# A recurrent state attention with two networks behind it on one core: transforms folded once more, the recurrence's heads laid out anew by partition halves

## The chip, the cores and the metric

One core of a Trainium2 chip runs the whole program. The metric is device time in microseconds (us). The engines are named as the profile names them: PE is TensorE's matmuls, PEld its weight loads, DVE is VectorE, ACT is ScalarE, POOL is GpSimd, SP is SyncE, whose queue issues most of the DMAs here.

## What is computed

```python
# 4 batches x 8 heads, 768 tokens, head dimension 40: 32 independent recurrences
for t in range(768):
    y[:, :, t] = einsum('bhd,bhde->bhe', r_t, state)
    Sa = einsum('bhde,bhe->bhd', state, a_t)
    state = state * w_t[:, :, None, :] - einsum('bhd,bhe->bhde', Sa, b_t) + einsum('bhd,bhe->bhde', v_t, k_t)
x = y, as [4, 768, 320]
# first network
u  = x + Re(FFT over tokens and features of x)
un = (u - mean(u)) / sqrt(var(u) + 1e-6)
x  = u + relu(un @ w_ch1) @ w_ch2                      # 320 -> 1280 -> 320
# second network
u  = x + transpose(relu(transpose(x) @ w_tok1) @ w_tok2)  # tokens 768 -> 256 -> 768
out = u + relu(u @ w_ch1) @ w_ch2                      # 320 -> 1536 -> 320
```

Precision is float32. Many products are made of high and low parts of the operands (names that end in `h` and `l`), as several matmuls that add up in one PSUM tile.

## The kernel before

**The recurrence.** The 768 tokens are cut into 12 superchunks of 64. Within a superchunk the recurrence becomes a triangular system for each of the 32 heads: `load`, `decay` (two scans on VectorE) and `kg` (score products, masked, written to `RT` and `LT`) prepare it. For each pair of superchunks, called a round here (6 in all), `inv` inverts the 32x32 triangular diagonal blocks of both superchunks at once on VectorE, with one block on each of 128 partitions: products (line 349) and reductions (line 350) over blocks of 8, 16 and 32. The blocks come from `RT` by way of DRAM: `RT` to `Gd`, `Gd` to the tile `N`. The result `Mt` goes to DRAM as `Md`, and its transposed form `MT`, which ScalarE makes, as `Ad`; they come back as `Mst` (four pieces a superchunk) and `AT`. `merge` joins the two 32-blocks of each head with 32x32 matmuls (`mg`, line 391, and `mc`, line 401) and ScalarE copies.

The serial part is `chain`, once a superchunk. 64 matmuls give `x` from `LT` and `RT` (line 450). Copies by VectorE and ScalarE put it into the block-diagonal tile `bdX`, two heads side by side, in four half-width pieces. 32 matmuls with all 128 rows (as the trace counts them, two for each call of the code) give the solve `z` from `Mst` and `bdX` (line 462). From it follow the new state, which is added to `LT`, and the next superchunk. `outp` makes the outputs of the superchunk and stores them. `wdec` decodes weights beside all this, and small matmuls called `warm` (line 55), whose result nobody reads, are put into TensorE's idle time.

**The Fourier layer.** For each batch, `fft` adds and subtracts mirrored tokens on VectorE (`F`, one folding) and transforms 3 token tiles with `psA` (line 868). `fft2` makes the transform over features, added up as `mix`: 6 tiles of 128 tokens, each 8 matmuls of 320 columns (line 895). Statistics, normalisation and transpositions follow.

**The networks.** They run in groups of 3 token tiles (384 tokens), 8 groups a network. For each of 10 (12) pieces `m` of the hidden width, `hps` is the first product (line 961, 8 matmuls of 384 columns), ScalarE and VectorE turn it into `hh` and `hl`, and `acc` is the second product (line 951, 9 matmuls of 320 columns). The token mixing of the second network is `tok` and `tok2`. Weights arrive packed; DVE, ACT and POOL decode them, the pieces are stored to DRAM (`dr_...`) and loaded again as `k` (first network) and `v` (second) from GpSimd's queue.

**The order.** The program is one list of operations with their dependences, and `Plan.emit` writes out the order on every engine before anything runs. Each operation has an estimated cost and a key, `lst`: the least, over its successors, of their key less (latency + cost) times `SLACK`; some operations have a due time as well, and `OFF` adds an offset for each stage (`inv`, `chain`, `decode` and so on) and for each of its instances. Smaller keys go first. At each step the engine whose next operation can start earliest takes, among those that could start within 0.25 us of that, the one with the least key. PSUM banks are dealt out by the same list: in the networks 2 banks `mm`, 3 `acc` and 3 `ps`.

## Time and profile before

| what | value |
|---|---|
| median of 3 runs | 994.69 us (993.87 to 1008.61) |
| profiled execution | 995.55 us |
| its span | 993.9 us, 24531 instructions |
| PE busy | 961.6 us (97%) |
| PEld busy | 924.0 us (93%) |
| DVE busy | 608.8 us (61%) |
| ACT busy | 420.5 us (42%) |
| POOL busy | 312.3 us (31%) |

The span is the time from the first to the last instruction of the profiled execution; its own time also holds what lies around that. A busy share is an average over stages that are limited by different things, so the rows below are taken by stage. `warm` counts as busy time of PE.

### The profile page before, as it was taken

The page shows a single profiled execution, that of the slowest core. Times are in us where ns is not written, and L with a number is a line of the kernel's source. Part 1 is how long each engine was busy: PE and PEld are TensorE (multiplying, and loading weights), DVE is VectorE, ACT ScalarE, POOL GpSimd, SP SyncE. Part 2 cuts the span into 40 slices and gives each one's busy share as a digit, 9 for nine tenths or more (in the row PEclk, how much of TensorE's full clock was granted, in tenths as well). Part 3 has the DMA queues.
Part 4 walks back from the last instruction along what each step waited for, and adds up shares of the span by engine and source line. Part 5 has one row for each costly group of instructions (what it writes and reads, how often), then busy time and mean ns, then how long its engine had stood idle before and what let it go on. Part 6 is the DMA issues. An engine that isn't in the chain of part 4 may idle for free. (4 is left out here: it accounts for less than half of the span.)

```text
span 993.9 us, 24531 instructions
## 1 busy us (share of the span) xinstructions
PE 961.6 (97%) x10119; PEld 924.0 (93%) x10119; DVE 608.8 (61%) x1364; ACT 420.5 (42%) x870; POOL 312.3 (31%) x427
## 2 busy tenths in 40 slices
PE   9998999999999899999999999999999999999998
PEld 8897788888888799899999999999999999999998
DVE  5699669888786159997798677626252522332322
ACT  4357787775857465423433333214131211221221
POOL 6754567663733255321215244420000000000000
PEclk9999999998999799999999999999999999999999
DMA  9996887889696777631325345491000000000000
GB/s 205 198 224 122 199 213 184 194 222 196 166 211 149 206 189 250 228 116 51 101 87 164 121 132 175 124 403 57 1 20 1 20 1 20 22 20 1 21 21 20
DMA packets 128722, 125.61 MB, mean 126 GB/s; under 512 B 85059, under 2 KB 105987, under 8 KB 128483
## 3 DMA queue, kind: packets, MB, share of 16 engines
q1 hardware_dynamic: 123715, 100.38, 40.0%
q0 software_dynamic: 4896, 23.67, 6.9%
q8 instruction: 79, 1.29, 0.6%
q14 instruction: 32, 0.26, 0.1%
HBM read 85.40 MB, written 33.84 MB: 120 GB/s over the span
## 5 line engine op out<-in xcount | busy, mean ns | idle before, releaser
L964 DVE SCALAR_TENSOR_TENSOR hl<-hps,hh 128x384 fp32r<-128x384 f32 x176 | 98.0, 557 | 234.1 <-ACT hh L963 233.1
L963 ACT ACTIVATE hh<-hps 128x384 fp32r<-128x384 f32 x176 | 86.5, 491 | 320.1 <-PE hps L961 320.0
L961 PE MATMUL hps<-th,v 128*128 128x384 f32 x576 | 142.5, 338 | 0.0
L951 PE MATMUL acc<-v,hh 128*128 128x320 f32 x576 | 128.8, 310 | 0.0
L961 PE MATMUL hps<-th,W 128*128 128x384 f32 x480 | 119.4, 339 | 0.1
L951 PE MATMUL acc<-W,hh 128*128 128x320 f32 x480 | 107.4, 310 | 0.6 <-DMA W<-m11l 0.6
L961 PEld LDWEIGHTS hps<-th,v 128*128 128x128 f32 x576 | 103.8, 188 | 0.2
L951 PEld LDWEIGHTS acc<-v,hh 128*128 128x128 f32 x576 | 97.9, 188 | 0.0
L829 POOL TENSOR_TENSOR mda<-mda,mdh 128x320 f32<-128x320 f32 (+2 forms) x44 | 45.4, 1037 | 149.2 <-DVE mdt L827 84.4
L951 PE MATMUL acc<-v,hl 128*128 128x320 f32 x288 | 89.0, 309 | 0.0
L961 PEld LDWEIGHTS hps<-th,W 128*128 128x128 f32 x480 | 86.8, 188 | 1.3 <-DVE hl L964 0.6
L951 PEld LDWEIGHTS acc<-W,hh 128*128 128x128 f32 x480 | 81.2, 188 | 0.8 <-DMA W<-m11l 0.8
L55 PE MATMUL warm<-ident 128*128 128x128 f32 x590 | 74.4, 282 | 3.0 <-POOL Q L237 2.0
L55 PEld LDWEIGHTS warm<-ident 128*128 128x128 f32 x590 | 70.3, 196 | 4.3 <-POOL Q L237 2.0
L951 PE MATMUL acc<-W,hl 128*128 128x320 f32 x240 | 73.9, 308 | 0.0
L961 PE MATMUL hps<-tl,v 128*128 128x384 f32 x192 | 64.6, 337 | 0.0
L521 PE MATMUL sc<-rm,VZd 120*128 120x192 f32 x264 | 54.2, 345 | 2.7 <-DVE sc L526 1.7
L951 PEld LDWEIGHTS acc<-v,hl 128*128 128x128 f32 x288 | 54.1, 188 | 0.0
L961 PE MATMUL hps<-tl,W 128*128 128x384 f32 x160 | 53.9, 337 | 0.0
L531 POOL TENSOR_SCALAR_AFFINE_SELECT sc<-sc 64x384 f32<-64x384 f32 (+1 forms) x72 | 38.6, 540 | 47.8 <-ACT sc L233 45.5
L311 PE MATMUL kg<-am,bt 120*128 120x192 f32 x242 | 50.2, 346 | 3.5 <-issue 1.8
L521 PEld LDWEIGHTS sc<-rm,VZd 120*128 120x128 f32 x264 | 43.0, 194 | 6.8 <-DVE sc L526 3.0
(176 smaller groups left out, 2025.0 us busy)
## 6 DMA issues: line engine op xcount, KB each, us to landing
bt<-in_bkR_dram SPq DMA_DIRECT2D x12, 660.0 KB
mdraw<-in_moe_w_ch_dram SPq DMA_DIRECT2D x22, 320.0 KB
wS<-in_wR_dram SPq DMA_DIRECT2D x12, 335.2 KB
a<-in_aR_dram SPq DMA_DIRECT2D x12, 335.2 KB
RT<-a SPq DMA_DIRECT2D x36, 111.7 KB
...
```

The costliest lines, as they stand in the source:

```text
L55: for x in range(m): nc.tensor.matmul(t[:,128*(x%4):128*(x%4)+128],lhsT=ident,rhs=ident,start=True,stop=True)
L311: nc.tensor.matmul(ps[:,192*x:192*x+192],lhsT=bt[:,g+x].rearrange("p v t -> p (v t)"),rhs=am[:,:,g+x],start=True,stop=True)
L521: for x,g in enumerate(gs): nc.tensor.matmul(ps[:,192*x:192*x+192],lhsT=VZd[:,g].rearrange("p v t -> p (v t)"),rhs=s.rm[:,:,g],start=True, ...
L531: nc.gpsimd.affine_select(out=o,in_=o,pattern=[[0,3*m],[1,L]],compare_op=ALU.is_gt,fill=0.0,base=0,channel_multiplier=-1)
L829: P.op('POOL',.06+d*.0025,lambda: nc.gpsimd.tensor_tensor(out=g("da").bitcast(F32),in0=g("da").bitcast(F32),in1=g("dh").bitcast(F32),op=AL ...
L951: nc.tensor.matmul(s.pst(acc[x]),lhsT=a[:,sl],rhs=t[w2][w][:,m],start=(m==0 and n==0),stop=(m==MT-1 and n==2))
L961: for n,(l,r) in enumerate(ops): nc.tensor.matmul(ps,lhsT=l,rhs=r,start=n==0,stop=n==7)
L963: s.act(384,lambda: nc.scalar.activation(out=t["hh"][z],in_=s.pst(h),func=AF.Relu),[kp],[('hh',z)],free=[h[0]])
L964: s.dve(.47,lambda: nc.vector.scalar_tensor_tensor(out=t["hl"][z],in0=s.pst(h),scalar=0.0,in1=t["hh"][z].bitcast(F32),op0=ALU.max,op1=ALU. ...
```

## The change

**The Fourier layer.** The token transform is folded twice: the tokens are kept in an order (`TOK`) in which the second mirror also falls on whole tiles, so that 2 token tiles go in and not 3. The feature transform is made for 161 frequencies only, cosine and sine sums side by side: 4 blocks a batch, each 2 matmuls of 384 columns and 6 of 192. The sums and differences that give both mirrored halves are made on VectorE (`DE`). The rows of `w_tok1` and `w_tok2` and the output are permuted on the host to fit.

**The networks.** They run in 6 chunks of 4 tiles (512 tokens), which may hold tiles of two batches (`TILES4`). `acc` has 4 PSUM banks and `ps` 2, `hh` and `hl` have two buffers, `hps` has 512 columns. The transform, mixing and transposition of the following chunk are put in at the middle of a chunk (`mid`). The `k` weights are loaded before the `v` weights.

**The recurrence.** `Gd`, `Md`, `Ad`, `AT` and their DMAs go. Four DMAs a superchunk bring the blocks from `RT` straight into an on-chip tile `Gs`, and three 32x32 block transpositions a round on VectorE give `N` and both forms of the result. `merge` of both superchunks stands right behind `inv`. Each half of the partitions holds 16 heads of both superchunks. `X1` takes the place of `bdX`: two full-width copies in place of four half-width ones, and the solve `z` is 64 matmuls (counted the same way) of 64 rows and 40 columns, which alternate between the upper and the lower 64 rows. Superchunks 0, 1, 6 and 7 are stored in reversed order of time, tables are smaller, and one buffer of `sc` goes.

**The order.** `SLACK` goes from 34.66 to 8 and every offset in `OFF` to 0; the planner's costs get an estimate of instruction fetch and of the hand-over of PSUM tiles, and new DMA constants.

```diff
-SLACK=34.6615
+SLACK=8.0000
+ROW={0:65,1:1,6:449,7:385}
...
+        s.X1,=mk(c2,1,[128,32,D],"X1"); s.Mst=mk(c2,2,[128,32,L],"Mst")
+        s.B,=mk(c2,1,[128,32,32],"B")
...
+        s.N,=mk(e,1,[128,32,32],"N"); s.Mt,=mk(e,1,[128,32,32],"Mt"); s.Gs,=mk(e,1,[128,32,32],"Gs")
...
-        s.Gd=mk(dr,2,[2,2,32,32,32],"Gd"); s.Md=mk(dr,2,[2,2,32,32,32],"Md"); s.Ad=mk(dr,2,[2,32,32,32],"Ad")
...
-        R=i//2
+        R=i//2; x=i%2
         for b in range(2):
-            s.dma(s.Gd[R%2][i%2,b].rearrange("n j t -> j n t"),RT[32*b:32*b+32,0:32,32*b:32*b+32],k6,[('Gd',R%2,i%2,b),('RTg',i%NRT,b)],.9)
-        q=32*(i%4)
-        s.act(.97,s.B[q:q+32],RT[0:32,0:32,32:64],k6,[('B',i%4),('RTg',i%NRT,2)],q=(0,q) if q else 0)
-        x=i%2
-        s.dma(s.N[64*x:64*x+64],s.Gd[R%2][x].rearrange("b n j t -> (b n) j t"),[('Gd',R%2,x,b) for b in range(2)],[('N',x)],.85)
+            for v in range(2):
+                q=64*v+32*b
+                s.dma(s.Gs[q:q+32,16*x:16*x+16],RT[32*b:32*b+32,16*v:16*v+16,32*b:32*b+32],k6,[('Gs',x,b,v),('RTg',i%NRT,b)],.5,ext=-.2)
+        for v in range(2):
+            s.act(.5,s.B[64*v:64*v+32,16*x:16*x+16],RT[0:32,16*v:16*v+16,32:64],k6,[('B',i%2,v),('RTg',i%NRT,2)],q=(0,64*v) if v else 0)
 
...
+        P.op('DVE',1.1,lambda: V.transpose(out=n(0,[1,32],[32,32]),in_=view(s.Gs,0,[1,32],[32,32])),[('Gs',x,b,v) for x in range(2) for b in range(2) for v in range(2)],NK+['S3'],lk=1)
...
-        s.act(.9,s.MT,s.Mt.rearrange("p i j -> p j i"),mk,['MT'])
-        for x in range(2):
-            s.dma(s.Ad[R%2][x],s.MT[64*x:64*x+32],['MT'],[('Ad',R%2,x)],.42)
-        s.dma(s.Md[R%2].rearrange("s b n i t -> (s b n) i t"),s.Mt,mk,[('Md',R%2)],1.69)
+        P.op('DVE',1.1,lambda: V.transpose(out=n(0,[1,32],[32,32]),in_=mm(0,[32,32],[1,32])),mk,NK+['S3'],lk=1)
+        P.op('DVE',1.1,lambda: V.transpose(out=view(s.Mst[R%2],32,[1,32],[L,32]),in_=mm(0,[1,32],[32,32])),mk,[('M',2*(R%2)),('M',2*(R%2)+1)],lk=1)
...
+        nc=s.nc; P=s.P; R=i//2; x0=16*(i%2); Mst=s.Mst[R%2]; B=s.B; km=('M',i%4); kt=('Tm',i%2)
+        for v in range(2): q=64*v; s.act(.48,Mst[q:q+32,x0:x0+16,0:32],Mst[q:q+32,x0:x0+16,32:64],[km],[('Mc',i%4,v)],q=(q,q) if q else 0)
+        mc=[('Mc',i%4,v) for v in range(2)]
+        for nm in range(2):
+            h=s.psum('c',[128,16,32],("mg","mc")[nm]); kp=('ps',h[0])
+            for k in range(0,16,4):
+                def f(k=k,h=h,nm=nm):
+                    ps=s.pst(h)
+                    for n in range(k,k+4):
+                        for v in range(2):
+                            q=64*v+32*nm; z=x0+n
+                            nc.tensor.matmul(ps[64*v:64*v+32,n],lhsT=B[q:q+32,z],rhs=Mst[q:q+32,z,32:64] if nm else s.N[q:q+32,z],start=True,stop=True,skip_group_check=True)
+                P.op('PE',.255,f,([kt,km] if nm else [('B',i%2,v) for v in range(2)]+['S3'])+([kp+(0,)] if k else []),[kp+(k,)]+([] if nm else [kt]),alloc=h[0] if k==0 else None,cols=512,ni=32,q='D')
+            for v in range(2):
+                q=64*v; o=Mst[q:q+32,x0:x0+16,32:64] if nm else B[q+32:q+64,x0:x0+16]
+                s.act(.48,o,lambda v=v,h=h: s.pst(h)[64*v:64*v+32],[kp+(k,) for k in range(0,16,4)]+(mc if nm else []),[km if nm else kt],free=[h[0]],q=(q,q+32-32*nm) if q+32-32*nm else 0)
 
...
-                    n=16*u+x; p=64*(n%2)
+                    n=16*(x%2)+8*u+x//2; p=64*(x%2)
...
+            P.op('PE',.967,f,rt+[('LTv',i%2)]+[('LT',i%2,x) for x in range(4)],[kp,('X1',i%2,u)],alloc=h[0],due=T0+PERIOD*i,cols=1280,ni=64,q='B')
+            o=s.X1[:,x0+8*u:x0+8*u+8]
+            if u==0 or i==0: s.act(.32,o,lambda h=h: s.pst(h),[kp],[('X1',i%2,u)],free=[h[0]])
+            else: P.op('DVE',.4,lambda o=o,h=h: nc.vector.tensor_copy(out=o,in_=s.pst(h)),[kp],[('X1',i%2,u)],free=[h[0]])
...
+            h=s.psum('c',[128,8,D],"z"); kp=('ps',h[0])
             def f(w=w,h=h):
                 ps=s.pst(h)
-                for x in range(4):
-                    for v in range(2): m=8*w+4*v+x; nc.tensor.matmul(ps[64*v:64*v+64,x],lhsT=Mst[:,m],rhs=s.bdX[:,m],start=True,stop=True,skip_group_check=True)
-            P.op('PE',.56,f,ms+[('bdX',w,hp) for hp in range(2)],[kp]+[('VZ',x) for x in ((0,8,11),(16,22,24))[w]],alloc=h[0],cols=2560,q='Z')
...
-            if i%2==1: go(i//2,'inv')
+            if i%2==1: go(i//2,'inv'); go(i-1,'merge'); go(i,'merge')
...
-     'decode': -11904.6, ('decode', 0): 23481.4, 'fft': 7216.7, ('fft', 0): 1641.4, ('fft', 1): 1161.5, ('fft', 2): 3067.5, ('fft', 3): -7083.3,
+     'decode': 0.0, ('decode', 0): 0.0, 'fft': 0.0, ('fft', 0): 0.0, ('fft', 1): 0.0, ('fft', 2): 0.0, ('fft', 3): 0.0,
...
+TOK=np.concatenate([128-np.arange(128),[0],np.arange(129,384),512-np.arange(128),[384],np.arange(513,768)])
...
-MB=dict(mm=2,acc=3,ps=3)
+MB=dict(mm=2,acc=4,ps=2)
...
+NHB=2
+TILES4=[[divmod(4*c+x,6) for x in range(4)] for c in range(6)]
...
+                if b or g:
+                    for j in (0,2): s.dve(lk=1,cost=.4,fn=lambda j=j,par=par: V(out=t["gh"][:,j],in0=t["F"][:,0],in1=t["F"][:,1],op=(ALU.add,ALU.subtract)[(j//2+par)%2]),R=[('F',0),('F',1)],W=[('gh',j)])
...
+                        seq=[y+((k,1-k)[tb//2],) for o,tb in blocks for k in range(*KK[tb//2]) for y in (("Xh",o,tb,k),("Xh",o,tb+1,k),("Xl",o,tb,k))]
+                        for n,(xx,o,tb,k,r) in enumerate(seq):
+                            nc.tensor.matmul(ps[:,c0:c0+cn],lhsT=t[xx][:,k,o:o+128],rhs=s.at.T1[:,r,tb,c0:c0+cn],start=n==0 and g==0,stop=n==len(seq)-1 and g==len(G)-1)
+                    s.pe((.336,.336,.672)[m]*w,f,rk+[('T1',k) for k in range(2)],[('psA',hs[m][0],par),('psb',hs[m][0])]+[('A',a) for a in ((0,1),(2,3),(4,))[m]],alloc=hs[m][0] if par==0 and g==0 else None,cols=(582,582,1164)[m]*w,ni=(6,6,12)[m]*w)
...
+        for c,sl in ((0,(0,5)),(1,(1,)),(2,(2,3)),(3,(4,))):
+            h=s.psum('mm',[128,2,FW],"mix"); kp=('pm',h[0]); j=s.nf%2; s.nf+=1
+            def f(h=h,c=c):
+                A=t["A"]; T2=t["T2"]; ps=s.pst(h).rearrange("p a f -> p (a f)"); q=slice(128*c,128*c+128); E=(slice(0,FW),slice(FW,2*FW)); W=slice(0,2*FW)
+                ops=[(A[4],2,128,W),(A[4],3,64,W)]+[y for e in range(2) for y in ((A[2*e],0,128,E[e]),(A[2*e],1,128,E[e]),(A[2*e+1],0,128,E[e]))]
+                for n,(aa,tb,K,w) in enumerate(ops):
+                    nc.tensor.matmul(ps[:,w],lhsT=aa[:K,q],rhs=T2[:K,tb,w],start=n==0,stop=n in (4,7),skip_group_check=True)
+            s.pe(1.03,f,[(('Am',a) if c==3 else ('A',a)) for a in range(5)]+[('A',a) for a in range(5)]+['T2','pend'],[kp],alloc=h[0],cols=1920,ni=16)
+            de=lambda j=j: t["DE"][j]
+            s.act(161,lambda h=h,j=j: nc.scalar.activation(out=t["DE"][j][:,1,:161],in_=s.pst(h)[:,1,:161],func=AF.Copy),[kp,'pend'],[('DE',j,1)],free=[h[0]])
+            for y in range(2): s.dve(.24,lambda h=h,j=j,y=y,de=de: V.tensor_tensor(out=de()[:,y,:161],in0=s.pst(h)[:,0,:161],in1=de()[:,1,:161],op=(ALU.subtract,ALU.add)[y]),[kp,('DE',j,1)],[('DE',j,y)],free=[h[0]])
+            xk=[y for i in sl for y in (s.at.xb(i,b) if s.first[b] else [])]+[('x',i,b) for i in sl]
+            n=len(sl); st=sl[-1]-sl[0] or 1; y0=c//3
+            xs=lambda lo,hi,sl=sl,st=st: s.at.X[:,sl[0]:sl[-1]+1:st,b,lo:hi]
+            dk=[('DE',j,y) for y in range(2)]
+            s.dve(.07+.168*n,lambda xs=xs,de=de,n=n,y0=y0: V.tensor_tensor(out=xs(0,161),in0=xs(0,161),in1=view(de(),162*y0,[162,n],[1,161]),op=ALU.add),(dk if n==2 else [dk[y0]])+xk,[('x',i,b) for i in sl])
+            s.dve(.07+.166*n,lambda xs=xs,de=de,n=n,y0=y0: V.tensor_tensor(out=xs(161,320),in0=xs(161,320),in1=view(de(),162*(1-y0)+159,[-162,n],[-1,159]),op=ALU.add),(dk if n==2 else [dk[1-y0]])+xk,[('x',i,b) for i in sl])
...
+            s.pe(1.756,f,[('hh',z),('hl',z)]+k2(m),[('acc',a[0]) for a in acc],alloc=[a[0] for a in acc] if m==0 else None,cols=3840,ni=24)
...
+            s.pe(1.868,f,tk+k1(m),[kp,('hh',z),('hl',z)],alloc=h[0],cols=3840,ni=16)
+            s.act(512,lambda: nc.scalar.activation(out=t["hh"][z],in_=s.pst(h),func=AF.Relu),[kp],[('hh',z)],free=[h[0]])
+            s.dve(.61,lambda: nc.vector.scalar_tensor_tensor(out=t["hl"][z],in0=s.pst(h),scalar=0.0,in1=t["hh"][z].bitcast(F32),op0=ALU.max,op1=ALU.subtract),[kp,('hh',z)],[('hl',z)],free=[h[0]])
...
+        go(s.fft2,0); t1(0)
+        def mid(c):
+            if c in (0,2,3): go(s.fft2,(c+2)//2+(c==3))
+            if c<5: t1(c+1)
+            if c==4: s.begin2()
+        for c in range(6):
+            stage(c)
+            if c in (0,1,3): go(s.fft,(c+3)//2)
+            stage(c)
+            s.ch(c,J[c],"W1","W2",10,k1,k2,s.fin1,lambda: (mid(c),stage(c)))
```

## Rows read from the trace of the kernel before

**Rows 1.** Busy time by stretch: start:end, length, PE, PEld, DVE, ACT, POOL, PEclk, DMA, GB/s

```profile
0.00:396.00 396.00, 369.63 (x6286) 335.63 (x6287) 292.66 (x615) 258.12 (x499) 220.77 (x325) 0.98 0.82 195
396.00:677.00 281.00, 278.88 (x1833) 275.87 (x1832) 208.43 (x504) 93.71 (x226) 91.54 (x102) 1.00 0.48 158
```

**Rows 2.** Busy time by stretch, line 55 (`warm`) alone: PE, PEld, PEclk, DMA, GB/s

```profile
0.00:396.00 396.00, 74.08 (x589) 70.18 (x590) 0.98 0.82 195
```

**Rows 3.** Busy time by stretch, the first network

```profile
404.00:640.00 236.00, 234.05 (x1551) 231.93 (x1550) 189.08 (x459) 81.21 (x194) 77.08 (x80) 1.00 0.40 123
```

**Rows 4.** Timeline of TensorE, first and last of 36 `psA`: start, us, operation

```profile
404.06 0.36 PE L868 MATMUL psA<-T,Xh 128*128 128x194 f32 x2
...
407.94 0.27 PE L868 MATMUL psA<-T,Xl 128*128 128x194 f32 x1
```

**Rows 5.** Chain of work that ended last: start, us, engine, operation, line, count

```profile
515.79 4.97 PE mix L895 x32
...
528.97 2.79 PE hps L961 x16
531.76 2.63 PE acc L951 x18
```

**Rows 6.** Timeline of all engines, first inverse: start, us, operation, [idle before, releaser]

```profile
37.94 0.45 SPq L231 DMA_DIRECT2D N<-Gd  x1
...
43.81 0.39 ACT L351 ACTIVATE it<-N 128x256 f32<-128x256 f32 x1 [5.30 <-DMA N<-Gd]
...
67.01 1.20 DVE L350 TENSOR_REDUCE Mt<-pr 128x32 f32<-128x512 f32 x2
...
80.26 1.20 PE L391 MATMUL mg<-AT,B 32*32 32x32 f32 x64
...
85.46 0.77 PE L462 MATMUL z<-bdX,Mst 128*64 128x80 f32 x16
```

**Rows 7.** Groups of VectorE, 405 to 994 us: busy us, mean ns, idle before

```profile
L849 DVE TENSOR_TENSOR F<-X 128x960 f32<-128x960 f32 x4 | 4.6, 1152 | 0.1
```

**Rows 8.** Instructions of the tile `MT`: ns least/median/most, stretch, shape

```profile
L233 ACT ACTIVATE MT<-Mt x6: 2021/2030/2047, 68.2 to 307.3; 128x1024 f32<-128x1024 f32 x6
```

**Rows 9.** Groups of VectorE, 0 to 396 us

```profile
L455 DVE COPY bdX<-x 64x320 f32<-64x320 f32 x22 | 10.7, 494 | 20.3 <-ACT bdX L233 14.8 <-PE x L450 5.2
```

**Rows 10.** Timeline of TensorE, solves and merges of the recurrence

```profile
145.98 1.33 PE L462 MATMUL z<-bdX,Mst 128*64 128x80 f32 x32
...
235.36 1.20 PE L401 MATMUL mc<-Mst,T 32*32 32x32 f32 x64
...
257.60 2.06 PE L450 MATMUL x<-LT,RT 128*64 128x40 f32 x64
...
327.54 1.20 PE L391 MATMUL mg<-AT,B 32*32 32x32 f32 x64
...
365.43 1.31 PE L462 MATMUL z<-bdX,Mst 128*64 128x80 f32 x32
```

**Rows 11.** Busy time of VectorE in line 349 alone, then in line 350 alone

```profile
0.00:396.00 396.00, 63.95 (x132) 0.98 0.82 195
...
0.00:396.00 396.00, 65.01 (x132) 0.98 0.82 195
```

**Rows 12.** Busy time by stretch, the steady part of the recurrence

```profile
60.00:306.00 246.00, 230.63 (x4281) 206.31 (x4279) 204.23 (x425) 176.89 (x328) 137.71 (x190) 0.99 0.82 190
```

**Rows 13.** DMA issues of `Mst`: queue, operation, count, size of one

```profile
Mst<-Md SPq DMA_DIRECT2D x48, 64.0 KB
```

**Rows 14.** Timeline of TensorE, an earlier solve, its first half

```profile
129.81 0.72 PE L462 MATMUL z<-bdX,Mst 128*64 128x80 f32 x16
```

**Rows 15.** Last load of `v` and first use: timeline, DMA issues (last: us to landing), timeline

```profile
652.89 0.53 POOL L800 DMA_DIRECT2D v<-dr_v1l  x1 [0.46 <-DMA k<-dr_k2h]
...
v<-dr_v1l POOLq DMA_DIRECT2D x3, 768.0 KB, 13.2
...
693.06 0.34 PE L961 MATMUL hps<-th,v 128*128 128x384 f32 x1
```

More of the change, by code (lines that the diff above doesn't have):

```diff
@@ L106, in pe @@
         return t
+    def pe(s,t,o):
+        w=o.cost; c=o.cols/w; n=s.count; s.count=n+o.ni
+        if o.ni and n+o.ni>s.page:
+            x=w*(s.page-n)/o.ni; t=max(s.work(t,x,c),s.avail); w-=x
+            s.page+=FETCH[0]; s.dma+=FETCH[2]; s.avail=max(s.dma,t+TURN)+LAND+FETCH[3]
+        return s.work(t,w,c)
     def emit(s,end,slack):
-        s.cols={}; s.hist=[]
+        s.cols={}; s.hist=[]; s.dma=s.avail=0.0; s.count=0; s.page=FETCH[1]
         ops=s.ops
@@ L181, in emit @@
             if o.lk: lock=o.fin
+            for h in o.tiles: touch.setdefault(h,{})[e]=o.fin
             s.trace.append((t,o))
@@ L682 @@
 HT=3300.0
+FW=192
 def round12(x):
@@ L947, in f @@
             def f():
-                for x in range(3):
+                for x in range(4):
                     sl=slice(128*x,128*x+128)
```

480 lines of the change are left out of this document (222 added, 258 removed), and 8 rows, old and new, of the table OFF.

## The prediction

> **What bounds the kernel now.** I read the busy time by stretch first [rows 1]. The run falls in two. Up to about 396 us stands the recurrence: TensorE is busy 369.6 of 396 us, VectorE 292.7, the DMA engines 82%, but 74 us of TensorE's busy time is `warm`, filler that computes nothing [rows 2]. So no engine is full there; the stage is a weave of serial steps. From 396 us to the end stand the Fourier layer and the two networks, and there TensorE has 2.1 us of idle time in the 281 us of the first network [rows 1]. That stage is as long as its matmuls. What is removed from TensorE there comes off the end one for one, unless another engine becomes late; VectorE is busy 189.1 of 236 us in the first network and is the one to watch [rows 3].
>
> The profiled execution took 995.55 us: a span of 993.9 us and 1.65 us around it. The median of the three timed runs is 0.86 us lower. I sum against 995.55 and take 0.86 off at the end.
>
> **Matmuls of the Fourier layer.** Durations in a pipelined stream are the spacing of many, not the 0.27 us of one [rows 4]. The token transform: 36 matmuls of 192 to 194 columns start between 404.06 and 407.94 us, 35 spacings in 3.88 us, 0.111 us each [rows 4]. A batch has 72 of them now (3 token tiles, 12 products, 2 parities) and 48 after the second fold. Three batches lie in the matmul-bound stage: 72 x 0.111 = 8.0 us less. Batch 0's 24 lie before 396 us beside filler, and I count them at nothing (2.7 us if that cover were gone). The channel transform: 32 matmuls in 4.97 us, 0.155 each [rows 5]; 4 batches x 6 x 8 = 192 make 29.8 us. After, each of 4 blocks a batch has 2 matmuls of 384 columns (0.174 us each by the chain's 16 in 2.79 us [rows 5]) and 6 of 192 (0.111): 1.015 us, 16 blocks, 16.2 us. That is 13.6 us less.
>
> **Chunks of 512 tokens.** The second product keeps its 1584 matmuls of 320 columns (18 in 2.63 us [rows 5]), and the transpositions keep their 144. The first product goes from 1408 of 384 columns to 1056 of 512. No row shows 512 columns. If the fixed part stays what it is, the step from 320 to 384 columns (0.146 to 0.174 us) gives 0.43 ns a column, 0.230 us at 512 and 2.9 us less in all; if time goes with columns, 0.233 us and nothing. I take 1.5 less, between near ends. Sum for this stage: 8.0 + 13.6 + 1.5 = 23.1 us less.
>
> **What may be given back there.** Chunk 1 now holds two tiles of batch 0 and two of batch 1, so batch 1's transform, mixing, statistics and transposition must be done within chunk 0 (10 x (1.84 + 1.76), 36 us) and not within two groups of three tiles (54 us). In 404 to 640 us VectorE is 80% busy [rows 3], and the same work is asked of it in a shorter time, with two `hh` buffers in place of three and one `mm` bank lent to the transform. `hl` of a step has 3.6 us of other matmuls as cover; where it queues behind weight decoding it waits for up to a few short operations. The new order puts decoding ahead: the offset that held it back is gone. I take 5 us of TensorE waits, between 0 and 15.
>
> **The recurrence.** Three things change length. First, the DMA hops around the inverse go. In round 0 the landing of `Gd` lets the SP queue issue `N` at 37.94 us, and the inverse starts at 43.81 [rows 6]. After, one hop of the first kind leads to a transposition on VectorE, so the 5.87 us of the second hop become one such operation. No row has a transposition; 1024 elements a partition at the rate of the flat 128x960 add (1.152 us [rows 7]) make 1.2 us, and by the scattered ScalarE copy of the same block (`MT`, 2.03 us [rows 8]) 2.0. VectorE and a flat write are nearer: 1.2. Gain 4.7. Then the inverse's last reduction ends at 68.2 and the first `mg` starts at 80.26 us [rows 6]: 12.1 us, replaced by two transpositions and hand-overs, some 3. Gain 9. So the first `z`, at 85.46, comes 14 us earlier. At the other end the same hop goes ahead of superchunk 10, but its `x` stands in the way, so I take 4 us there.
>
> Second, VectorE gets 18 transpositions, 21.6 us (up to 36.5), and loses one of two half-width `bdX` copies in 11 steps: 22 x 0.49 = 10.7 us now [rows 9], half after: net 16.3 us on 292.7. Whether that costs anything depends on what sets the pace. The solves go from 85.46 to 365.43 us [rows 6, 10], 11 steps, 50.9 us a pair. Of the inverse's own work 63.95 + 65.01 us [rows 11], 21.5 a round, all on VectorE. If VectorE sets the pace at its share of 83% (204.2 of 246 us from 60 to 306 [rows 12]), 2.6 us more a pair cost 3.2, over 5.5 pairs 17 us. If the DMA queue sets it, the cost is nothing, and the queue is relieved: each round now writes `Md` and reads it in eight `Mst` pieces [rows 13], beside `N`, `Ad` and `AT`.
>
> Third, the solve itself. `z` goes from 32 passes of 80 columns to 64 of 40 (1.33 us now [rows 10]). With `x`'s spacing, which has the same 64-column weights and 40 columns, it takes 2.06 us; with `mc`'s, whose weights alternate between row groups, 64 in 1.20 us [rows 10]. I take 2.06 as the nearer shape: 0.73 a step, 8.8 in all, on a path that has slack in most steps, 3 us of it felt. The Trainium skill, TensorEngine Tiling (Array Packing), "Gotcha 1: PSUM Pressure", says that different row tiles cannot access one PSUM bank at the same time, and the two halves of `z` write one bank. By that rule the halves take turns and 2.06 stands; without it 1.27 would do and the sum would be 3 us lower. The trace doesn't settle it: `mc` (alternating row groups, one bank) and `mg` (one row group) both take 1.20 us for 64 [rows 10].
>
> Moved and small edits. The `merge` step goes from its own superchunk to right behind the inverse: 64 small matmuls twice and six ScalarE copies a superchunk, past the work of up to two superchunks on both queues; its matmuls (1.2 us each [rows 10]) run in TensorE's filler time, and the SP queue loses the waits for `Md` and `AT`. The eight `k` loads go ahead of the `v` loads on GpSimd's queue; one that waits for its decoded piece holds up the decoding operations queued behind it there, by a store's landing of some us, with VectorE two jobs ahead. The reversed storage of four superchunks, smaller tables, one `sc` buffer less and fewer memsets I cost at nothing: transfers and GpSimd work beside a stage in which no engine is full; without that cover 1 to 3 us.
>
> The order decides the rest. It comes from a key, path length to the end times `SLACK`, plus offsets that are now all zero. By the code's costs an inverse's first operation ranks with the superchunk 5 to 6 steps ahead of the one it feeds, its last with the one just before, so inverses push in front of the chain's evacuations for part of each round. Between 0 for a weave as good as today's and 42 (the slower rival), I take 8 us for pace and order together beyond those 3: 11 us. Recurrence: -14 - 4 + 11 = 7 us less. Sum: 995.55 - 23.1 + 5 - 7 = 970.45, 969.6 against the median; I say 970.
>
> **Rivals.** (a) Slower than before: the inverse and the chain exclude one another on VectorE. Then a pair takes 21.5 + 3.6 + small copies, some 26, plus two steps at the fastest seen, 129.81 to 145.98 us, 16.2 each [rows 10, 14]: 58.6 in place of 50.9, 42 us over 5.5 pairs; with 15 us of waits in the networks: 995.55 - 23.1 + 15 - 18 + 42 - 0.86 = 1010.6. For it: the key above. Against it: a step needs VectorE for only some 3 of its 16 us. With those 15 us of waits it eats the gains up from 4.8 us a pair on. (b) Faster: the shorter lag lets VectorE run at 92% where 83% is seen; (42.3 + 2.6)/0.92 = 48.8 a pair, 11.5 less, 12 less at the tail since both last merges come early, 2 us of waits: 995.55 - 23.1 + 2 - 14 - 12 - 11.5 - 0.86 = 936. (c) The second network waits for its weights: now the last `v1` load is issued at 652.89 us, right after decoding, and takes some 13.2 us to land, against a first matmul at 693.06 [rows 15]. That matmul comes at about 669 after; the load, four us earlier without the `k` loads in front, would land at 662 if decoding ends when it does now. It decides if decoding ends more than 7 us later, as it may with less idle VectorE; 15 us later gives 8 us, 978. Against it: decoding ranks higher now. (d) The fold doesn't remove what it says, being paid back by the new additions on VectorE: then the networks' stage keeps its length and 988 follows.
>
> **Chances.** Forecast 0.46 (own range 955 to 984), (a) 0.20, (b) 0.17, (c) 0.08, (d) 0.09. A measurement of this kernel tells about 2% from no change. Faster by over 2% (below 974.8): most of the forecast and (b), 0.53. Within 2%: the rest of it, (c), (d) and the half of (a) whose waits are smaller, 0.38. Slower by over 2%: (a) with a pair above 59 us, 0.09. The range takes in (b) and most of (a): 932 to 1006.
>
> **What would show it.** Right: 144 `psA` matmuls for batches 1 to 3, `mix` blocks of about 1.0 us, TensorE idle in the networks under 10 us, first `z` near 71 us, `mix` of batch 0 near 389 us. Wrong: pairs of `z` 58 us apart with inverse operations back to back; TensorE waiting for `hl`; first `hps<-v` waiting for a DMA; `z` at 1.3 us for 64 passes (the halves overlap). Most likely to spoil it: the order in the recurrence.

## The result: 1.0% slower

The changed kernel takes 1004.81 us in the median of 20 runs (998.95 to 1011.73), the kernel before 995.33 in 20 runs beside it (986.72 to 1011.15). The ratio is 1.0102, 95% interval 1.0079 to 1.0126. I had said 970 us, 2.5% faster: the time lies inside my range, on the other side of no change.

The profiled execution has a span of 1000.4 us, 6.5 more than before. Busy time by stretch comes first, as in [rows 1, 12]. The columns are the same.

```profile
0.00:396.00 396.00, 365.94 (x6510) 331.64 (x6511) 314.23 (x615) 252.91 (x502) 228.64 (x327) 0.96 0.67 159
...
396.00:677.00 281.00, 280.24 (x1709) 251.92 (x1709) 209.62 (x518) 88.97 (x221) 86.39 (x98) 1.00 0.48 157
...
60.00:311.00 251.00, 240.14 (x4742) 215.27 (x4743) 220.19 (x424) 190.16 (x369) 149.03 (x206) 0.99 0.62 143
```

The DMA engines fell from 82% to 67% in the recurrence, as the edits meant. VectorE rose from 83% to 88% of the steady part, and the granted clock fell from 0.98 to 0.96. The first network looks as full as before (280.24 of 281 us), but part of that is now filler. The line of `warm` alone, by stretch, first in the changed kernel, then in the kernel before:

```profile
401.00:684.00 283.00, 20.45 (x168) 19.35 (x167) 1.00 0.45 149
```

```profile
400.00:677.00 277.00, 0.00 (x0) 0.00 (x0) 1.00 0.48 154
```

So a full TensorE no longer means that the stage is as short as its matmuls: 20.45 us of it are matmuls that nobody reads. From the first `mix` to the end, first in the changed kernel, then in the kernel before:

```profile
401.00:1000.40 599.40, 595.23 (x3512) 539.42 (x3511) 305.26 (x674) 151.89 (x330) 84.46 (x95) 1.00 0.23 77
```

```profile
396.00:993.90 597.90, 592.01 (x3835) 588.32 (x3833) 316.18 (x751) 162.42 (x372) 91.54 (x102) 1.00 0.25 81
```

VectorE, the third busy time, has less to do there than before, 305.26 us against 316.18. From the first `mix` to the first product it stays nearly full, and the stretch keeps its length (changed kernel, then before):

```profile
401.00:418.70 17.70, 17.19 (x134) 15.38 (x134) 15.93 (x51) 5.73 (x15) 2.52 (x3) 1.00 0.62 232
```

```profile
396.10:414.50 18.40, 17.10 (x131) 16.17 (x131) 16.89 (x56) 8.40 (x24) 5.52 (x6) 1.00 0.76 269
```

Before, TensorE had the second batch's transform to do meanwhile [rows 4]; now some 10 us of the 20.45 us of filler stand here. The start of the first solve (timeline), the tile `mix` (ns least/median/most, first and last start):

```profile
79.08 1.13 PE L466 MATMUL z<-X,Mst 64*64 64x40 f32 x32
```

```profile
L916 PE MATMUL mix<-T,A x128: 272/276/443, 401.0 to 596.2; 128*128 128x192 f32 x96, 128*128 128x384 f32 x16, 64*128 64x384 f32 x16
```

The chain of work that ended last shows the new durations, against [rows 4 to 6, 10]:

```profile
32.61 5.92 DMA Gs<-RT
...
70.91 1.94 PE mg L405 x112
...
370.91 1.99 PE z L466 x64
...
418.95 3.73 PE hps L985 x16
...
435.30 2.66 PE psA L893 x24
...
447.91 2.79 PE mix L916 x16
```

24 `psA` in 2.66 us are 0.111 each, as before; a batch has 48 and not 72. 16 `hps` of 512 columns in 3.73 us are 0.233 each. A `mix` block of 8 takes 1.395 us, where I had 1.015. The transpositions, new on VectorE, are the groups of that engine up to 400 us:

```profile
L367 DVE STREAM_TRANSPOSE N<-Gs 128x1024 f32<-128x1024 f32 x6 | 12.7, 2113 | 4.0 <-DMA RT<-a 3.3 <-DMA Gs<-RT 0.7
L389 DVE STREAM_TRANSPOSE N<-Mt 128x1024 f32<-128x1024 f32 x6 | 11.9, 1978 | 0.0
L390 DVE STREAM_TRANSPOSE Mst<-Mt 128x1024 f32<-128x1024 f32 x6 | 11.7, 1957 | 0.0
```

18 of them cost 36.3 us, 2.0 each. Against my terms (the start of the first `mix` parts the recurrence from the networks):

| term | predicted, us | in the profile |
|---|---|---|
| token transform | -8.0 | -8.0 (24 x 3 matmuls fewer) |
| feature transform | -13.6 | -7.5 (16 blocks x 1.395 = 22.3, before 29.8) |
| first product | -1.5 | 0 |
| waits in the networks | +5 | +17 (what is left of that stage's length, 597.8 to 599.4 us) |
| first solve | -14 | -6.4 (85.46 to 79.08 us) |
| tail of the recurrence | -4 | -0.4 (last `z` to first `mix`, 30.6 to 30.2 us) |
| pace and order of the recurrence | +11 | +11.8 (first `z` to last, 280.0 to 291.8 us) |

They add up to +6.5, the difference of the spans, as they must: the waits in the networks are what is left over. No term came out better than I had it, and the first and the last are by number as I had them. One mechanism late in the recurrence, within the pace term, shows what a loss by order can look like: the timeline of all engines, superchunk 10.

```profile
339.41 1.13 PE L466 MATMUL z<-X,Mst 64*64 64x40 f32 x32
...
343.66 0.33 DVE L834 TENSOR_SCALAR mdt<-mdraw 128x320 int32<-128x320 int32 x1 [7.58 <-DMA mdraw<-in_moe_w_ch_dram]
...
344.43 0.55 DVE L530 TENSOR_TENSOR sc<-sc,tri 128x384 f32<-128x384 f32 x1
...
346.36 0.67 PE L543 MATMUL y<-Sbd,r 120*64 120x120 f32 x4 [5.82 <-DVE ys L563]
...
348.60 1.93 PE L466 MATMUL z<-X,Mst 64*64 64x40 f32 x32
```

VectorE stands for 7.58 us at a decoding operation whose DMA is not there. An output operation behind it (`sc`) could have run; `y` waits for what follows from that, and the second half of the solve is queued behind `y`. TensorE stood idle for 5.82 us before `y`, and then ran at its lower level. In the busy time by stretch the granted clock is the third number from the right:

```profile
340.00:350.00 10.00, 4.18 (x70) 3.98 (x68) 3.29 (x9) 3.69 (x7) 3.19 (x5) 0.61 0.94 256
350.00:360.00 10.00, 10.00 (x125) 8.98 (x124) 2.50 (x6) 4.23 (x10) 3.85 (x6) 0.50 0.86 221
```

0.50 of full speed is 1.2 GHz. Nothing in the edits asks for this wait; it is where the order put one operation. It is not new in kind: in the kernel before TensorE stood idle in the same superchunk, ahead of `x`, and its granted clock then fell too, for a shorter time.

```profile
334.28 2.79 PE L450 MATMUL x<-LT,RT 128*64 128x40 f32 x47 [3.38 <-issue]
```

```profile
330.00:340.00 10.00, 6.62 (x136) 6.25 (x135) 0.99 (x2) 2.67 (x6) 0.00 (x0) 0.67 0.91 193
340.00:350.00 10.00, 9.76 (x174) 8.78 (x173) 2.81 (x7) 4.56 (x11) 3.38 (x6) 0.82 0.19 57
```

What the wait costs is tried below.

### The profile page after: what moved, and what is told of

It reads as the page before. It is cut to its first block, busy times and chain, and to the rows that moved or that the text cites. A ratio compares the mean times of both kernels' runs of the same rounds, so it can differ in the third digit from the quotient of the medians.

```text
span 1000.4 us, 24233 instructions
## 1 busy us (share of the span) xinstructions
PE 966.2 (97%) x10065; PEld 876.1 (88%) x10065; DVE 624.3 (62%) x1307; ACT 408.4 (41%) x847; POOL 315.0 (31%) x425
## 4 chain that ended last, share of the span: by engine, by line
PE 75%; DVE 12%; DMA 5%; ACT 3%; issue 3%; POOL 1%; SPq 1%; DVEq 0%; POOLq 0%; ACTq 0%
PE hps L985 24%; PE acc L975 23%; PE kg L327 3%; PE warm L59 3%; DVE pr L365 2%; PE sc L525 2%; PE tps L1049 2%; PE t2ps L1062 2%; PE mix L916 2%; PE psA L893 2%; PE z L466 1%; DMA RT<-a 1%; PE trp L956 1%; PE y L547 1%; DVE it L366 1%
## 5 line engine op out<-in xcount | busy, mean ns | idle before, releaser
L988 DVE SCALAR_TENSOR_TENSOR hl<-hps,hh 128x512 fp32r<-128x512 f32 x132 | 91.1, 690 | 233.9 <-ACT hh L987 233.6
L987 ACT ACTIVATE hh<-hps 128x512 fp32r<-128x512 f32 x132 | 78.9, 598 | 325.3 <-PE hps L985 325.1
L985 PE MATMUL hps<-th,v 128*128 128x512 f32 x432 | 135.0, 396 | 0.0
L985 PE MATMUL hps<-th,W 128*128 128x512 f32 x360 | 113.0, 396 | 0.0
L985 PEld LDWEIGHTS hps<-th,v 128*128 128x128 f32 x432 | 81.1, 188 | 16.8
L59 PE MATMUL warm<-ident 128*128 128x128 f32 x664 | 86.1, 284 | 2.0 <-POOL Q L254 2.0
L985 PEld LDWEIGHTS hps<-th,W 128*128 128x128 f32 x360 | 67.6, 188 | 13.6
L985 PE MATMUL hps<-tl,v 128*128 128x512 f32 x144 | 57.0, 396 | 0.0
L340 POOL TENSOR_SCALAR_AFFINE_SELECT RT<-RT 64x384 f32<-64x384 f32 (+1 forms) x72 | 43.5, 634 | 27.7 <-ACT RT L250 26.6
L327 PEld LDWEIGHTS kg<-am,bt 120*128 120x128 f32 x242 | 41.1, 200 | 12.5 <-ACT am L250 8.0
```

The source lines that it names most:

```text
L59: for x in range(m): nc.tensor.matmul(t[:,128*(x%4):128*(x%4)+128],lhsT=ident,rhs=ident,start=True,stop=True)
L327: nc.tensor.matmul(ps[:,192*x:192*x+192],lhsT=bt[:,g+x].rearrange("p v t -> p (v t)"),rhs=am[:,:,g+x],start=True,stop=True)
L340: nc.gpsimd.affine_select(out=kv,in_=kv,pattern=[[0,n],[1,L]],compare_op=ALU.is_gt,fill=0.0,base=0,channel_multiplier=-1)
L985: for n,(l,r) in enumerate(ops): nc.tensor.matmul(ps,lhsT=l,rhs=r,start=n==0,stop=n==7)
L987: s.act(512,lambda: nc.scalar.activation(out=t["hh"][z],in_=s.pst(h),func=AF.Relu),[kp],[('hh',z)],free=[h[0]])
L988: s.dve(.61,lambda: nc.vector.scalar_tensor_tensor(out=t["hl"][z],in0=s.pst(h),scalar=0.0,in1=t["hh"][z].bitcast(F32),op0=ALU.max,op1=ALU. ...
```

## The experiments

My theory after reading the two traces, **order**: the edits are worth about what I said, and what was lost is the order that the old kernel's offsets gave it. The first rival, **load**: the edits themselves cost the time, by the transpositions on VectorE and the dearer mixing. Where a result is one execution, without an interval, I read only its trace. Three profiled executions with the same recurrence have their first `mix` at 401.0, 402.6 and 403.5 us, so such times differ by some 3 us without a cause in the program.

### The old kernel without its offsets

```diff
-SLACK=34.6615
+SLACK=8.0000
...
-     'decode': -11904.6, ('decode', 0): 23481.4, 'fft': 7216.7, ('fft', 0): 1641.4, ('fft', 1): 1161.5, ('fft', 2): 3067.5, ('fft', 3): -7083.3,
+     'decode': 0.0, ('decode', 0): 0.0, 'fft': 0.0, ('fft', 0): 0.0, ('fft', 1): 0.0, ('fft', 2): 0.0, ('fft', 3): 0.0,
...
```

> The kernel before, with the changed kernel's ordering parameters and nothing else of the change: every offset of the order at 0 and SLACK 8. Theory 'order' (the edits are worth their time, and what was lost is the order that the offsets gave): the old kernel without its offsets is 25 to 40 us slower, 1020 to 1035 us, ratio 1.025 to 1.04 to the kernel before. Theory 'load' (the edits themselves cost the time, by three transpositions a round on VectorE and dearer mixing): the old kernel keeps within 8 us of its time, ratio under 1.008.

1029.69 us, ratio 1.0322 (1.0254 to 1.0391), 34 us above the 995.84 us of the kernel before beside it. That is what the offsets and the larger `SLACK` were worth to the old kernel together; the run changes both. The tile `mix` says where:

```profile
L895 PE MATMUL mix<-T,A x192: 302/308/412, 429.0 to 645.3; 128*128 128x320 f32 x192
```

The first `mix` starts at 429.0 us in place of 396.1, so 33 of the 37.5 us of span lie in the recurrence. With these ordering parameters on both sides (the cost tables of the two planners still differ) the changed kernel is 22 us the faster one (1.0102 against 1.0322). By the spans of the profiled executions it is 31 us: its recurrence ends 28 us earlier (401.0 against 429.0), and its networks are only 3 us shorter (599.4 against 602.4).

### The changed kernel with offsets of its own

`OFF` filled with values from a random search that asks only the kernel's own planner; no instruction is changed.

> The changed kernel, not an instruction of it altered, with offsets for its stages found by some 25,000 random steps against the kernel's own planner, which then puts its end 23.8 us earlier (941.8 in place of 965.6). Theory 'order': most of that is real, 15 to 25 us shorter, 980 to 990 us, ratio to the kernel before 0.985 to 0.995, with the gain in the recurrence and in the filler of the first network. Rival 'edits': the loss is in longer operations and an order moves it only about; within 6 us of the changed kernel, ratio 1.004 or more.

982.95 us, ratio 0.9894 (0.9841 to 0.9946): by the ratios 21 us below the changed kernel, as the theory has it. The tile `mix` of this kernel, its busy time by stretch at the times shown above, and its filler from the first `mix` on:

```profile
L912 PE MATMUL mix<-T,A x128: 272/276/443, 386.0 to 572.6; 128*128 128x192 f32 x96, 128*128 128x384 f32 x16, 64*128 64x384 f32 x16
```

```profile
340.00:350.00 10.00, 10.00 (x240) 8.95 (x237) 5.45 (x11) 6.04 (x13) 6.81 (x9) 1.00 0.87 228
350.00:360.00 10.00, 9.90 (x133) 8.52 (x130) 5.05 (x11) 6.30 (x16) 4.83 (x8) 1.00 0.82 237
```

```profile
386.00:976.00 590.00, 8.23 (x64) 7.63 (x64) 1.00 0.24 79
```

The first `mix` comes at 386.0 us, 15 earlier; the end of the recurrence runs at full clock. The networks take 590.0 us in place of 599.4, with 8.23 us of filler in place of 20.45. The profiled execution is the fastest of the six (977.68 us), so some of this is that execution.

### Every transposition twice

```diff
-P.op('DVE',1.1,lambda: V.transpose(out=n(0,[1,32],[32,32]),in_=mm(0,[32,32],[1,32])),mk,NK+['S3'],lk=1)
+P.op('DVE',1.1,lambda: (V.transpose(out=n(0,[1,32],[32,32]),in_=mm(0,[32,32],[1,32])),V.transpose(out=n(0,[1,32],[32,32]),in_=mm(0,[32,32],[1,32]))),mk,NK+['S3'],lk=1)
...
```

> The changed kernel with each of the 18 transpositions on VectorE issued twice in a row (the second repeats the first), order unchanged: 36 us more of VectorE work in the recurrence. Theory 'load': VectorE sets the pace, and 25 to 36 us come on top, ratio 1.035 to 1.046. Theory 'order': VectorE has slack in most rounds, and only the rounds in which the inverse is late pay: under 12 us, ratio under 1.022.

1041.01 us, ratio 1.0444 (1.0378 to 1.0510), by the ratios 34 us more than the changed kernel for 36.3 us of work.

```profile
L916 PE MATMUL mix<-T,A x128: 271/276/443, 431.0 to 626.2; 128*128 128x192 f32 x96, 128*128 128x384 f32 x16, 64*128 64x384 f32 x16
```

The first `mix` moves from 401.0 to 431.0 us. So the rival holds as well in its own place: in this order nearly all the time that was added to VectorE in the recurrence came on at the end. The two theories do not exclude each other; the load is real, and an order decides how much else is lost beside it. That less work would give its time back in the same way is not shown; the next run has a case in which it did not.

### The pattern of a transposition

```diff
-P.op('DVE',1.1,lambda: V.transpose(out=n(0,[1,32],[32,32]),in_=view(s.Gs,0,[1,32],[32,32])),[('Gs',x,b,v) for x in range(2) for b in range(2) for v in range(2)],NK+['S3'],lk=1)
+P.op('DVE',1.1,lambda: V.transpose(out=n(0,[32,32],[1,32]),in_=view(s.Gs,0,[32,32],[1,32])),[('Gs',x,b,v) for x in range(2) for b in range(2) for v in range(2)],NK+['S3'],lk=1)
```

> The changed kernel, the first transposition of a round with both sides read and written flat, block by block, which transposes other 32x32 blocks than wanted (the inverses and all that follows from them are then other numbers). Theory 'pattern': the 2.11 us of this operation come from the elements 32 apart, and flat it takes 1.1 to 1.2 us. Rival 'operation': VectorE's transposition goes at 2 ns an element whatever the pattern, and it stays at 2.0 to 2.1 us.

```profile
L367 DVE STREAM_TRANSPOSE N<-Gs 128x1024 f32<-128x1024 f32 x6 | 7.4, 1231 | 4.3 <-DMA RT<-a 4.3
```

1.23 us flat, 2.11 with elements 32 apart on both sides: the pattern is the price. My 1.2 us was right for an operation that the kernel doesn't have. The other two transpositions kept 1.96 to 1.97; one of them is flat on the side that it reads, so a strided write alone has that price, and a strided read alone was not tried. The flat row keeps the pace of the flat add in [rows 7], 1.2 ns an element; the strided rows take 1.9 to 2.1 ns. The Trainium skill, Vector Engine (DVE) Microarchitecture Reference, section 3.8, says that the transposing array keeps up one element per cycle and lane. The flat row does not contradict it; what a strided pattern costs it leaves open.

The six faster transpositions take 5.3 us of work from VectorE in the recurrence, and yet the first `mix` of this one execution comes at 405.8 us, 4.8 later than in the changed kernel. So the time taken out was not seen at the end.

### The row of 64 in a mixing block

```diff
-ops=[(A[4],2,128,W),(A[4],3,64,W)]+[y for e in range(2) for y in ((A[2*e],0,128,E[e]),(A[2*e],1,128,E[e]),(A[2*e+1],0,128,E[e]))]
+ops=[(A[4],2,128,W),(A[4],3,128,W)]+[y for e in range(2) for y in ((A[2*e],0,128,E[e]),(A[2*e],1,128,E[e]),(A[2*e+1],0,128,E[e]))]
```

> The changed kernel; the one matmul of a mixing block that has 64 rows is given all 128 (the added rows of its table are zeros, so the sum is the same). Theory 'switch': a matmul of another height in the stream holds up its neighbours, so the block of 8 goes from 1.395 us to some 1.03, 16 blocks give back 5.9 us, ratio to the kernel before 1.004. Rival 'columns': the 384-column and 192-column matmuls themselves take longer here; the block stays at 1.39 us and the ratio at 1.010.

1001.63 us, ratio 1.0057 (1.0023 to 1.0090), by the ratios 4.5 us below the changed kernel, with intervals that overlap. The chain shows two blocks in a row:

```profile
482.08 2.02 PE mix L916 x16
```

1.01 us a block in place of 1.395; more rows are faster. 0.38 us a block, 6.1 us over 16, is what one matmul of 64 rows costs among those of 128. In the changed kernel the weight loads of a block (timeline of PEld) show where:

```profile
448.02 0.18 PEld L916 LDWEIGHTS mix<-T,A 64*128 64x128 f32 x1 [0.22 <-issue]
448.38 0.86 PEld L916 LDWEIGHTS mix<-T,A 128*128 128x128 f32 x7 [0.18 <-issue]
```

The weight loads pause for 0.22 us before the load of 64 rows and for 0.18 us after it; with 128 rows the 16 loads of two blocks follow one another without such a pause. The Trainium skill, TensorEngine Tiling (Array Packing), "Key Properties", says that changing the tiling mode drains TensorE. These rows agree, and it is the rule against the change that I should have weighed: the 64 stands in the diff.

### Offsets and the block together

> The same offsets, and the 64-row matmul of a mixing block given 128 rows as in the run before it. If the two act apart, 4 to 6 us below the run with the offsets alone: ratio 0.980 to 0.991. If the first network waits for VectorE and not for TensorE there, the shorter blocks turn into filler and nothing is gained.

975.49 us, ratio 0.9803 (0.9759 to 0.9847). The median is 7 us below the offsets alone, with intervals that overlap by a little, so the 4 to 6 us that were expected are not contradicted. The first solve, the last one and the first `mix`:

```profile
75.46 1.13 PE L466 MATMUL z<-X,Mst 64*64 64x40 f32 x32
```

```profile
351.39 2.06 PE L466 MATMUL z<-X,Mst 64*64 64x40 f32 x64
```

```profile
L912 PE MATMUL mix<-T,A x128: 250/274/446, 389.3 to 570.9; 128*128 128x192 f32 x96, 128*128 128x384 f32 x32
```

The networks take 585.0 us, 5.0 less than with the offsets alone.

### A second search, with the measured transposition

```diff
-P.op('DVE',1.1,lambda: V.transpose(out=n(0,[1,32],[32,32]),in_=mm(0,[32,32],[1,32])),mk,NK+['S3'],lk=1)
+P.op('DVE',1.92,lambda: V.transpose(out=n(0,[1,32],[32,32]),in_=mm(0,[32,32],[1,32])),mk,NK+['S3'],lk=1)
```

in all three places, with the block above and offsets searched again.

> The changed kernel with the 128-row mixing block, the planner told 2.0 us for each transposition in place of 1.18 (the traces show 1.96 to 2.11), and offsets searched again from there, some 55,000 steps more. If the wrong duration was what cost the recurrence its order, the plan now fits the chip and the time falls below the run with the first offsets and the same block: 960 to 972 us, ratio to the kernel before 0.967 to 0.978. Rival: a planner that is wrong by 0.8 us in 18 places was good enough, and two searches end alike, 972 to 980 us, ratio 0.978 to 0.986.

981.62 us, ratio 0.9881 (0.9850 to 0.9912): above both ranges that were expected, though its interval reaches into the rival's. A planner with better durations did not find the better order here. Its recurrence ends at 399.5 us in the profiled execution (987.9 us, the longest of its six). The clock is at 0.91 from 200 to 400 us where the best one has 0.93 and then 1.00. Two searches land 6 us apart by the medians, the later one behind.

### Second batch's transform first

```diff
-     'decode': 0.0, ('decode', 0): 0.0, 'fft': 0.0, ('fft', 0): 0.0, ('fft', 1): 0.0, ('fft', 2): 0.0, ('fft', 3): 0.0,
+     'decode': 0.0, ('decode', 0): 0.0, 'fft': 0.0, ('fft', 0): 0.0, ('fft', 1): -30000.0, ('fft', 2): 0.0, ('fft', 3): 0.0,
```

> The changed kernel with one offset: the second batch's transform is ranked ahead of all else, so its matmuls can run where filler stands from 407 to 419 us. Theory 'order': the 10.3 us of filler there give way to the 48 matmuls of batch 1, which go out of the first chunk; 5 to 8 us shorter, ratio 1.002 to 1.005. Rival 'VectorE late': the fold of batch 1 (0.8 + 0.9 us and more) then stands ahead of the statistics of batch 0 on VectorE, the first product starts later by as much as the filler saved, within 2 us, ratio 1.010.

1014.36 us, ratio 1.0186 (1.0134 to 1.0238): a miss for the theory, beyond what even the rival gave it.

```profile
423.52 3.03 PE L916 MATMUL mix<-T,A 128*128 128x384 f32 x16 [0.28 <-DVE A L902]
...
426.39 3.31 PE L59 MATMUL warm<-ident 128*128 128x128 f32 x28
```

The filler only moves. The first `mix` itself comes 8.9 us later, at 409.9. The second batch is mixed early, at 423.52 us, and the first product starts at 437 us in place of 418.7: sums, splits and statistics of both batches now stand in one queue on VectorE, which is busy 23.26 of the 27.60 us from the first `mix` to the first product. In this order TensorE lacks VectorE's time there, and not other matmuls.

### Decoding behind all else

```diff
-     'decode': 0.0, ('decode', 0): 0.0, 'fft': 0.0, ('fft', 0): 0.0, ('fft', 1): 0.0, ('fft', 2): 0.0, ('fft', 3): 0.0,
+     'decode': 0.0, ('decode', 0): 5000.0, 'fft': 0.0, ('fft', 0): 0.0, ('fft', 1): 0.0, ('fft', 2): 0.0, ('fft', 3): 0.0,
```

> The changed kernel with one offset: the decoding of the networks' weights is ranked behind everything else that is ready. Theory 'VectorE late in the first network': 20.4 us of filler stand in that stage because statistics, sums and splits share VectorE with decoding; behind them, decoding leaves 12 to 14 us of filler, so 6 to 8 us shorter, ratio to the kernel before 1.002 to 1.004, with the recurrence as it was. Rival 'structure': the filler is set by the chain mix, statistics, transposition, whatever VectorE does beside it; within 2 us, ratio 1.010. A second network that waits for its weights would show as a wait for a DMA at its first product and could make it slower.

1000.69 us, ratio 1.0091 (1.0048 to 1.0134), which doesn't settle it against the changed kernel. The filler from the first `mix` on:

```profile
403.50:997.30 593.80, 13.29 (x108) 12.62 (x108) 1.00 0.23 78
```

It goes from 20.45 to 13.29 us, within the 12 to 14 that were expected, and the networks go from 599.4 to 593.8, 5.6 less where 6 to 8 were expected. The first `mix` came 2.5 us later in the profiled execution, before any operation that the offset concerns. So by the trace a third of the filler is owed to decoding. The second network did not wait for its weights.

### One wait of VectorE

```diff
-P.op('SP',.5,lambda sl=sl,sr=sr: nc.sync.dma_start(out=raw()[sl],in_=sr.bitcast(I32)),['mid' if j else 'mid0'],kr if len(src)==1 else [kr[x]],due=due,rel=rel,data=d*.0036,ext=-.3)
+P.op('SP',.5,lambda sl=sl,sr=sr: nc.sync.dma_start(out=raw()[sl],in_=sr.bitcast(I32)),['mid' if j else 'mid0'],kr if len(src)==1 else [kr[x]],due=due,rel=rel,data=d*.0036,ext=2.0 if nm=='w2' and n==1 else -.3)
```

> The changed kernel with one number of its planner altered: the landing of the second packed piece of w_ch2 is put 2.3 us later, so that on VectorE the piece's decoding stands behind one operation of the outputs where it stood ahead of it. Theory 'one wait': in the changed kernel VectorE stands 7.58 us at that decoding for its DMA (to 343.66 us), with a copy of the chain and an output queued behind it, and TensorE idles 5.8 us and runs at half clock to about 363; without it the first mixing starts at 391 to 396 us in place of 401. Rival 'elsewhere': the last superchunks are late for other reasons, and the first mixing stays within 2 us of 401. The order in the networks shifts too (the planner puts its end 8 us later), so the first mixing is compared and not the total.

```profile
L916 PE MATMUL mix<-T,A x128: 272/276/443, 400.6 to 603.4; 128*128 128x192 f32 x96, 128*128 128x384 f32 x16, 64*128 64x384 f32 x16
```

```profile
347.48 0.33 DVE L834 TENSOR_SCALAR mdt<-mdraw 128x320 int32<-128x320 int32 x1 [4.57 <-DMA mdraw<-in_moe_w_ch_dram]
```

400.6 us: by the mark I had set, the rival. But the `x` of superchunk 10 already started at 337.55 us in this execution and at 332.68 in the changed kernel's, so from there to the first `mix` it is 63.1 in place of 68.3 us. The wait shrank from 7.58 to 4.57 us and did not go, and from 350 to 360 us the clock was at 0.50 here too. What one wait cost stays open, between nothing and some 5 us.

### The row halves of a solve

Half by half in place of one by one, then each half in a PSUM bank of its own:

```diff
-for x in range(8):
-    for v in range(2): z=x0+8*w+x; nc.tensor.matmul(ps[64*v:64*v+64,x],lhsT=Mst[64*v:64*v+64,z],rhs=s.X1[64*v:64*v+64,z],start=True,stop=True,skip_group_check=True)
+for v in range(2):
+    for x in range(8): z=x0+8*w+x; nc.tensor.matmul(ps[64*v:64*v+64,x],lhsT=Mst[64*v:64*v+64,z],rhs=s.X1[64*v:64*v+64,z],start=True,stop=True,skip_group_check=True)
```

> The changed kernel with the matmuls of a solve in another order: all of the upper 64 rows first, then all of the lower, in place of one by one. If the two row halves overlap when they alternate, 64 passes go from 1.99 us to 2.5 or more. If they take turns anyway, the 64 passes keep 1.99 us within 0.1.

```diff
-h=s.psum('c',[128,8,D],"z"); kp=('ps',h[0])
+hs=[s.psum('c',[128,8,D],"z") for v in range(2)]; kps=[('ps',h[0]) for h in hs]
...
-    for v in range(2): z=x0+8*w+x; nc.tensor.matmul(ps[64*v:64*v+64,x],lhsT=Mst[64*v:64*v+64,z],rhs=s.X1[64*v:64*v+64,z],start=True,stop=True,skip_group_check=True)
+    for v in range(2): z=x0+8*w+x; nc.tensor.matmul(ps[v][64*v:64*v+64,x],lhsT=Mst[64*v:64*v+64,z],rhs=s.X1[64*v:64*v+64,z],start=True,stop=True,skip_group_check=True)
```

> The changed kernel with the two row halves of a solve in a PSUM bank each (half a solve then takes both banks of its pool, and the second half waits for copies of the first, so the whole may get slower). Theory 'bank': halves that write different banks run side by side, and 32 passes go from 1.15 us with their tail to 0.7 or less. Rival 'weights': each pass needs its own weight load, and loads set 31 ns a pass; 32 passes stay at 1.1 to 1.2 us.

Timelines of TensorE in the changed kernel, with half by half, and with two banks:

```profile
262.41 2.06 PE L466 MATMUL z<-X,Mst 64*64 64x40 f32 x64
```

```profile
216.47 3.30 PE L466 MATMUL z<-X,Mst 64*64 64x40 f32 x64
```

```profile
197.36 1.13 PE L466 MATMUL z<-X,Mst 64*64 64x40 f32 x32 [0.46 <-DVE X L460]
```

64 passes take 2.06 us in alternation and 3.30 one half after the other: passes that alternate overlap. Each row half also writes its own half of the partitions here, and no run parts the two; `x`, which uses all 128 rows and alternates only in the partitions that it writes, has 2.06 us for 64 as well [rows 10]. In a bank each, 32 passes take 1.13 us, as they do in one bank (79.08 us above). So the sentence of the Trainium skill on row tiles and one PSUM bank (TensorEngine Tiling (Array Packing), "Gotcha 1: PSUM Pressure"), which I had weighed in the prediction, shows no cost in these rows: two row halves that write one bank are not slower than two that write two. That each pass needs its own weight load, the rival of this run, fits 1.13 us; that the loads set the pace is not shown. The duration that I took from `x` was right, and the reason that I put beside it, halves taking turns, was not. And the solve's length is felt in full, as far as single executions can tell: 1.24 us more in 12 solves, 14.9 us, and the first `mix` moved from 401.0 to 417.35. These two are single executions of 1018.82 and 1025.67 us; the two-bank one also waits for its banks.

## Why the prediction was wrong

**The step that failed** is the price of the order. "The order decides the rest" stands in the prediction, but in the sum it is 8 us, all in the pace of the recurrence ("I take 8 us for pace and order together"), with 5 us of waits in the networks beside it. The trace of before came from an order with searched offsets, and I treated that weave as a property of the kernel that would pass to the new one. With the changed kernel's offsets and slack the old kernel loses 34 us (1.0322). With offsets of its own the changed kernel gains 21 (1.0102 to 0.9894), and with the mixing block mended as well it stands at 975.49 us.

By terms, the pace came out as written, and the loss lies where I had put little or nothing for the order: waits in the networks of 17 us for 5, so that the 15.5 us of matmuls removed there did not come "off the end one for one"; a first solve 6.4 us earlier for 14; a tail 0.4 us shorter for 4. With offsets of its own and the mended block, in the profiled execution of that run, the same terms are -10.0 for the first solve, -4.0 for the pace, +7.3 for the tail and +8.7 for the waits. So an order of its own gives back 16 us of pace and 8 us of waits, and lengthens the tail by 8.

Two sums near mine are luck. 975.49 us lies 5.5 from my number, with other terms than mine. And with default orders on both sides the changed kernel is 22 us faster, near the 25 us of my sum, but 28 of the 31 us between those spans lie in the recurrence and 3 in the networks, where I had 7 and 18.1.

**Right.** The token transform went as summed, 0.111 us a matmul. The block of `mix` is 1.01 us once its rows are equal, against my 1.015. The `z` of 64 passes takes 2.06 us as taken. The first product gained nothing, at one of the two ends that I had named; I took the middle. The 71 us for the first solve and 389 for the first `mix` were not reached by the changed kernel (79.08 and 401.0); the one with searched offsets came near the first and passed the second (74.35 and 386.0). "TensorE idle in the networks under 10 us" was a poor sign of being right: it came true (595.23 of 599.40 us busy) because filler counts as busy.

**Sizes that were off.** The mixing by 6.1 us, for the 64-row matmul. A transposition costs 2.0 us and not 1.2, 36.3 us in all, the upper bound that I had named. I had given VectorE's extra load and the solve's 0.73 us partial weight, "a path that has slack in most steps"; doubling the one and slowing the other showed almost all of the added time at the end. That pace and order still came out at 11.8 us, near the 11 that I had written, is not a confirmation: a dearer transposition and a fully felt solve should have cost more, so something else, perhaps the DMA queue that fell from 82% to 67%, gave some back. No run takes that apart.

**The start.** I had 4.7 us for the hop into the inverse and 9 for the hop out of it. The way in gained nothing (the inverse's first copy at 43.35 us against 43.81), since `Gs` took 5.92 us to land and VectorE was in a scan until 41.2 us. The way out gained 7.8 (66.5 to 70.8 us against 68.2 to 80.26). But merging both superchunks in one go costs 8.2 us from the first `mg` to the first `z`, against 5.2 [rows 6], with more ScalarE copies in between; I had not counted that. The inverse itself was 1.2 us shorter.

**The rivals.** (a) was too dark in its mechanism: a pair of solves takes 53.1 us, not 58.6. Its own sum, 1010.6, lay outside the range that I said takes in most of it. (b) did not come. (c) was nothing: the last `v1` loads are issued from 634.68 us on, and their first use is at 701.28. (d), at a chance of 0.09, is what the changed kernel shows in the networks by its outcome, 599.4 against 597.8 us. Its cause is not shown: VectorE has less to do there than before (305.26 us against 316.18). 15.5 us of matmuls were gained and 17 lost to waits; with decoding last there is 7.2 us less filler, with searched offsets 12.2 less, so at least that part is the order. What the rest of the 17 us is made of stays open.
